# First block of a fused kernel: a longer distance from h to y, weights converted two chunks ahead, three passes from earlier chunks on

## The chip, the cores and the metric

The kernel runs on one core of a Trainium2 chip. Its metric is the device time of one execution in microseconds. TensorE multiplies matrices, VectorE, ScalarE and GpSimd do the elementwise work, and SyncE (SP) issues every DMA. Each engine works through its own instructions in order and waits on semaphores for the others.

## The reference

An attention with keys and values averaged over groups of 8 positions, and two feed-forward layers behind it, all float32 (2304 rows, 512 wide, 2048 hidden):

```python
k_p = k.reshape(B, H, Sp, 8, D).mean(axis=3)      # v_p likewise
attn = softmax(q @ k_p.T / sqrt(D))               # B 4, H 8, S 576, D 64
x = (attn @ v_p) as (2304, 512)
h = x @ w_in                                      # 512 -> 2048
g = where(h >= 1, h, where(h <= -1, 0, (h + 1)**2 / 4))
x = g @ w_out                                     # 2048 -> 512
h = x @ w_in2;  g = max(h, 0) + log1p(exp(-abs(h)));  out = g @ w_out2
```

## The kernel before

The 18 tiles of 128 rows are cut into blocks of 4, 4, 4, 3 and 3 tiles (`BLK`). Attention of a block's tiles runs one block ahead, among the matmuls of the block before; that of block 0 stands in a list, `START`. In each block the first feed-forward layer runs over 16 chunks of 128 hidden columns. The loop at L811 is this layer: turn n is chunk c of block j, here called step c. It emits h(c) = w_in(c) x on TensorE (`emit_g1`), then the elementwise g, and y += w_out(c) g (`emit_g2`) some steps later. `pend` holds the chunks whose y is still to come; before the change y runs two chunks behind h. The h banks in PSUM are two, so h(c) needs min/max(c-2), the last reader of its bank.

`act` makes g: Relu and Square on ScalarE, then min/max on VectorE (L538). A chunk that is multiplied in three passes has g split besides: a high half (ScalarE, L546) and a low half (VectorE, L548).

A product is made either in one fp32 pass, or in three passes of halves rounded to fp32r: high x high, high x low, low x high. For three passes w, x or g has to be split. `HSPLIT` says from which chunk of block 0 h takes three passes, `GSPLIT` the same for y. The later blocks take three throughout. `split_x0` splits the x of block 0 in two parts, `split1` a weight piece (ScalarE first, VectorE a step later), `SPLITS` says in which step.

The weights come as 64-bit words. `convert1` turns one piece of two chunks' weights into fp32 in two parts: two ScalarE passes (`words`), then two on VectorE (`exponents`: a shift, L125, and a merge, L126) and one on GpSimd (`last_bits`, L132). `USE` is the order of the 16 pieces: w_in of chunks 0 and 1, w_in of 2 and 3, w_out of 0 and 1, w_in of 4 and 5, w_out of 2 and 3, and so on. `w_load` brings a piece by DMA, four steps ahead.

`background` adds what `plan` has for each half step hs = 2n and 2n+1: the k and v sums of the next batch (L348), their transposes (L399) and scaled copies (L355, L359), and the stages of an attention tile (`tile_gen`): scores, row minimum, exponentials, normalisation, transposes, product with v, copy into x. A "wide" tile subtracts the minimum on VectorE and has one exponential of 576 columns, others eight of 72. From CONV2 on `tick` adds the conversion of the second layer's weights. The order on each engine is the order in which this code is run.

Of the kernel before, what the change touches and what calls it, by code (L numbers as in the profile page):

```python
# [25 lines left out]
NC = DFF // 128  # L26
# [4 lines left out]
def pooled_attention_ffn_ffn(ctx, tc, q, k, v, v0, w1, w2, out):  # L31
# [11 lines left out]

    START = (
        "z z z z z k0 k1 k2 k3 q0 q1 q2 q3 v w0 w1 K0 K1 K2 K3 L A0 A1 A2 B0 E0 B1 E1 A3 V C0 B2 D0 "
        "B3 E2 E3 T0 C1 U W0 C2 D1 P0 C3 T1 X0 D2 P1 S0 T2 X1 D3 P2 F0 T3 X2 P3 X3 w2 W1 b w3"
    )


# [6 lines left out]
    )  # L56


    HSPLIT, GSPLIT = 8, 12
    CONV2, PITCH = 44, 3.1  # L60

    BUDGET = ((0.0, 0.0), (1.0, 2.5), (1.2, 2.5), (0.9, 1.9), (0.9, 1.9))
    T0 = [sum(BLK[:j]) for j in range(NB)]
# [46 lines left out]
    def slot(shape, dtype, name):  # L110
        return wpool.tile(shape, dtype, tag="w", name=name)
# [5 lines left out]
    def words(src, a, r):  # L117
        x = src.rearrange("p (f w) -> p f w", w=2)
        nc.scalar.activation(
            out=a.bitcast(FP32), in_=x[:, :, 1].bitcast(FP32), func=ACTF.Copy, scale=2.0 ** -112  # L120
        )
        nc.scalar.activation(out=r, in_=x[:, :, 0], func=ACTF.Copy, scale=2.0 ** -29)

    def exponents(a, b):
        nc.vector.tensor_scalar(out=b, in0=a, scalar1=3, scalar2=None, op0=ALU.logical_shift_left)  # L125
        nc.vector.scalar_tensor_tensor(  # L126
            out=a, in0=a, scalar=0x80000000, in1=b, op0=ALU.bitwise_and, op1=ALU.bitwise_or
        )

    def last_bits(a, r):  # L130
        a = a.bitcast(I32)
        nc.gpsimd.tensor_tensor(out=a, in0=a, in1=r, op=ALU.add)  # L132
# [10 lines left out]
    def convert1(m):  # L143
        a = slot([128, 2 * DM], U32, "wf")
        r = es2.cv.tile([128, 2 * DM], I32, tag="r", name="r")
        words(raw.pop(m), a, r)
        yield
        b = es2.cv.tile([128, 2 * DM], U32, tag="b", bufs=1, name="b")
        exponents(a, b)
        last_bits(a, r)  # L150
        wt[USE[m]] = a.bitcast(FP32).rearrange("p (h f) -> p h f", h=2)
        yield
        yield

    def split1(m):

        hi, lo = (slot([128, 2, DM], FP32R, n) for n in ("whi", "wlo"))
        f = wt[USE[m]]
        nc.scalar.activation(out=hi, in_=f, func=ACTF.Copy)
        yield  # L160
        nc.vector.tensor_tensor(out=lo, in0=f, in1=hi.bitcast(FP32), op=ALU.subtract)
        wt[USE[m]] = (hi, lo)
        yield

    def st_load(n):
        if n < 2 * NC:
            (part, h), r = USE[n // 2], n % 2
            raw[n] = es2.cv.tile([128, 2 * DM], U32, tag="st", name="st")
            landing.append([3, n])
            src = w2[part, h].bitcast(U32)[:, r * 2 * DM:(r + 1) * 2 * DM]  # L170
            nc.sync.dma_start(out=raw[n], in_=src)
# [167 lines left out]
    def kv_load(b, nm, p, ring=True):  # L339
        shape = [128, T * POOL]  # L340
        t = es2.cv.tile(shape, FP32, tag="kv", name="kv") if ring else slot(shape, FP32, "kv")
        nc.sync.dma_start(out=t, in_=k[b, p] if nm == "k" else v[b - 1, p])
        kst[b, nm, p] = t
# [13 lines left out]
    def v_done(b, pa):  # L357
        vps[b] = att.tile([T, DM], FP32, tag="vp", bufs=2, name="vp")
        nc.scalar.activation(out=vps[b], in_=pa[0:T, 0:DM], func=ACTF.Copy, scale=1.0 / POOL)  # L359
# [211 lines left out]
    def emit_y(j):  # L571
        n = 128 * BLK[j]
        t = xpool.tile([128, KD, TB], FP32, tag="xh", name="y")
        for m, y in enumerate(yacc.pop(j)):
            if m % 2:
                nc.vector.tensor_copy(out=t[:, m, 0:n], in_=y[:, 0:n])
            else:
                nc.scalar.activation(out=t[:, m, 0:n], in_=y[:, 0:n], func=ACTF.Copy)  # L578
        later.append((j, t))
# [97 lines left out]
    c1 = [convert1(m) for m in range(NC)]  # L677
# [39 lines left out]
    for op in START.split():  # L717
        n = int(op[1:] or 0)
        if op == "z":
            for _ in range(4):  # L720
                nc.tensor.matmul(out=zp, lhsT=zeros[:, 0:128], rhs=zeros, start=True, stop=True)
        elif op == "b":
            for nm in "kv":
                for p in range(NP):
                    kv_load(1, nm, p, ring=False)
        elif op == "v":
            v0_load()
        elif op == "V":
            vpa = v0_pool(ps_z.tile([128, 512], FP32, tag="zp", name="vpa"))
        elif op == "U":  # L730
            v_done(0, vpa)
        elif op == "L":
            k_done(0)
        elif op[0] == "k":
            kv_load(0, "k", n, ring=False)
        elif op[0] == "K":
            kv_pool(0, "k", n)
        elif op[0] == "w":
            w_load(n)
        elif op[0] == "q":  # L740
            q_load(n)
        elif op[0] in "WSF":
            next(c1[n])
        else:
            if op[0] == "A":
                tg[n] = tile_gen(n, 0, wide=n != 1)
            next(tg[n])
# [5 lines left out]


    def wide(i):
        return i >= T0[2] and i % 2 == 0

    plan = {}
    for j, counts in enumerate(KV_PLAN):
# [15 lines left out]
    def background(hs):  # L775
        credit[0] = min(credit[0] + BUDGET[hs // 2 // NC][hs % 2], 3.0)
        for key in plan.get(hs, ()):
            if key not in gens:
                gens[key] = (
                    kv_gen(key[1]) if key[0] == "kv" else x_gen(key[1]) if key[0] == "x"  # L780
                    else tile_gen(*key, wide=wide(key[0]))
                )
            credit[0] -= cost.get(key, 0.0)
            cost[key] = next(gens[key])
        if hs >= CONV2:
            todo = len(units)
            tick(hs >= due[0])
            due[0] += (len(units) < todo) * PITCH

    pend = []  # L790
    acts = {}
    SPLITS = {
        (0, 13): (14,),
        (0, 14): (15, 0),
        (0, 15): (1, 2),
        (1, 1): (3,),
        (1, 2): (4,),
        (1, 3): (5,),
        (1, 4): (6,),
        (1, 5): (8,),  # L800
        (1, 6): (10,),
        (1, 7): (12,),
    }
    splits = []

    def step(key):

        if key in acts:
            next(acts[key], None)

    for n in range(NB * NC):  # L811
        j, c = s = divmod(n, NC)
        hs = 2 * n
        hot = j == 0
        if s == (1, 0):
            esc.close()
            es2.cv = esc.enter_context(tc.tile_pool(name="cv2", bufs=2))
        acts[n] = act(emit_g1(j, c), j, c)
        pend.append(s)

        if hot and c + 2 < NC:
            next(c1[c + 2])
        if n > NC + 2:
            step(n - 2)
        step(n - 1)
        if j and c == 2:
            emit_y(j - 1)
        for g in splits:
            next(g)
        splits = []  # L830
        if n <= NC + 2:
            step(n - 2)
        if hot and c + 1 < NC:
            next(c1[c + 1])
        if hot and c in (HSPLIT - 2, HSPLIT - 1):
            xg = split_x0(c - HSPLIT + 2)
            next(xg)

        if hot and HSPLIT - 1 <= c < NC - 2 and c % 2:
            w0 = split1(c)  # L840
            next(w0)
        if hs == CONV2 - 4:
            st_load(0)
            st_load(1)
        background(hs)

        while later:
            y1_store(*later.pop(0))
        while len(pend) > 2:
            emit_g2(*pend.pop(0))  # L850
        step(n - 1)
        next(acts[n])
        if hot and c + 1 < NC:
            next(c1[c + 1])
        if hot and c + 4 < NC:
            w_load(c + 4)
        if hot and c in (HSPLIT - 2, HSPLIT - 1):
            next(xg, None)
        if hot and HSPLIT - 1 <= c < NC - 2 and c % 2:
            next(w0)  # L860
        background(hs + 1)

        if (j, c) in SPLITS:
            splits = [split1(m) for m in SPLITS[j, c]]
            for g in splits:
                next(g)
            credit[0] -= 1.2
        if j == LAST and c in (11, 12, 13, 14):
            for i in range(2):
                wi_load((c - 11) // 2, (c - 11) % 2 * 2 + i)  # L870
# [13 lines left out]
    NQ = NS * NH  # L884
    xg = None

    FILL = {0: (2, 2, 1, 1, 1, 1, 0), 1: (0, 0, 0, 0, 0, 0, 6), NQ - 1: (0,) * 7}

    def filler(n):
        for _ in range(min(n, len(fill))):  # L890
# [3 lines left out]
    for q in range(NQ):  # L894
# [7 lines left out]
        if m == 2 and s + 1 < NS:  # L902
            xg = x_gen(s + 1)
        for p, o in enumerate(banks[b] for b in PRODUCTS):
# [11 lines left out]
            if p == 6:  # L916
                act2(q, 1, hb)
            filler(FILL[q][p] if q in FILL else 2 if p < 5 else 1)
            while later:
# [49 lines left out]
```

## Time and profile before

| | us |
|---|---|
| median of 3 runs | 874.84 (874.32 to 874.99) |
| the profiled execution | 875.78 |
| its span, first to last instruction | 874.0 |
| TensorE busy in the span | 860.2 (98%) |
| VectorE, ScalarE, GpSimd busy | 580.9, 517.8, 86.8 |
| first block, from its first h to its last | 28 to about 136 |

Rows of the profile begin with a start and a duration, or with a stretch. In the windows every engine has busy time and count; behind them stand TensorE's granted clock (1.00 is full), the share of the DMA engines and GB/s. The names before and behind `<-` are tiles written and read; brackets at a row's end give the idle time ahead of it and what ended it. In the chain a piece of fp32 matmuls counts two records each. L numbers are lines of the kernel before.

### The profile page before, as it was taken

To read this page: it belongs to the slowest core of one execution; us is meant where nothing else is said; L and a number is where in the kernel's file an instruction comes from. 1 tells how busy PE (TensorE), PEld (TensorE's weight loads), DVE (VectorE), ACT (ScalarE), POOL (GpSimd) and SP (SyncE) were. 2 spreads that over 40 slices of the span, in tenths; PEclk is the share of its full clock that TensorE was granted. 3 is DMA by queue.
4 is the path that set the end of the run, shared out by engine and by line. 5 is a ranking of instruction groups with operands and counts; after the bars stand their busy time and mean duration, and the time that the engine had idled before them with its cause. 6 is when DMAs were issued, how large, how long until landed. Compare 5 with 4: busy or idle time off the path is not lost.

```text
span 874.0 us, 12211 instructions
## 1 busy us (share of the span) xinstructions
PE 860.2 (98%) x4538; PEld 721.9 (83%) x4538; DVE 580.9 (66%) x845; ACT 517.8 (59%) x931; POOL 86.8 (10%) x57
## 2 busy tenths in 40 slices
PE   8999999999999999999999999999999999999997
PEld 4445668888887888899999988998898989989886
DVE  6577666755576475667675487767687675765754
ACT  4877765565656665777674457455475554644552
POOL 0442330011111112112110000000000000000000
PEclk9999999999999999999999999999999999999999
DMA  7853401512386353754867395556296455596302
GB/s 265 331 181 150 157 13 42 177 37 89 121 273 212 126 169 109 241 176 140 275 235 240 116 340 181 165 171 252 89 392 214 115 177 217 184 353 198 94 1 73
DMA packets 65643, 154.94 MB, mean 177 GB/s; under 512 B 6128, under 2 KB 26608, under 8 KB 63536
## 3 DMA queue, kind: packets, MB, share of 16 engines
q1 hardware_dynamic: 65584, 154.17, 52.2%
q8 instruction: 36, 0.59, 0.3%
q14 instruction: 23, 0.19, 0.1%
HBM read 121.63 MB, written 32.51 MB: 176 GB/s over the span
## 4 chain that ended last, share of the span: by engine, by line
PE 91%; ACT 3%; DMA 3%; DVE 2%; issue 1%; SPq 0%; ACTq 0%
PE h L523 22%; PE y L564 22%; PE y L640 22%; PE h L603 19%; PE a L412 2%; PE a L470 2%; PE a L456 2%; DMA x<-y1d 1%; DMA st<-in_w 1%; DMA kv<-in_k 1%; ACT e L445 1%; PE vpa L374 1%; ACT pT L462 0%; DVE e L452 0%; DVE mn L431 0%
## 5 line engine op out<-in xcount | busy, mean ns | idle before, releaser
L603 PE MATMUL h<-xfh,wi 128*128 128x384 f32 x544 | 160.3, 337 | 1.9 <-DVE h L911 1.2
L640 PE MATMUL y<-whi,gl 128*128 128x512 f32 x288 | 114.2, 397 | 0.4 <-DVE gl L624 0.4
L523 PE MATMUL h<-xl,whi 128*128 128x512 f32 (+1 forms) x320 | 114.3, 373 | 0.0
L640 PE MATMUL y<-wlo,gh 128*128 128x512 f32 x288 | 113.7, 395 | 0.0
L640 PE MATMUL y<-whi,gh 128*128 128x512 f32 x288 | 112.0, 389 | 0.0
L603 PEld LDWEIGHTS h<-xfh,wi 128*128 128x128 f32 x544 | 100.8, 188 | 9.4 <-DVE h L911 2.6
L564 PE MATMUL y<-gh,whi 128*128 128x512 f32 (+1 forms) x272 | 100.9, 371 | 1.1 <-ACT y L578 1.1
L564 PE MATMUL y<-gl,whi 128*128 128x512 f32 (+1 forms) x272 | 99.0, 364 | 0.0
L564 PE MATMUL y<-gh,wlo 128*128 128x512 f32 (+1 forms) x272 | 98.9, 364 | 0.0
L523 PE MATMUL h<-xh,whi 128*128 128x512 f32 (+1 forms) x256 | 94.1, 368 | 0.0
L523 PE MATMUL h<-xh,wlo 128*128 128x512 f32 (+1 forms) x256 | 92.8, 362 | 0.0
L603 PE MATMUL h<-xfl,wi 128*128 128x384 f32 x272 | 91.8, 338 | 0.0
L614 ACT ACTIVATE e<-h 128x768 f32<-128x768 f32 x48 | 40.1, 840 | 84.9 <-DVE h L911 84.9
L532 ACT ACTIVATE t<-h 128x512 f32<-128x512 f32 (+1 forms) x80 | 44.3, 554 | 74.7 <-PE h L523 74.6
L911 DVE TENSOR_TENSOR h<-h,s 128x384 f32<-128x384 f32 x72 | 40.0, 555 | 65.5 <-PE h L603 65.1
L132 POOL TENSOR_TENSOR a<-a,st 128x512 int32<-128x512 int32 x32 | 47.4, 1483 | 275.5 <-DVE a L126 194.2
L538 DVE SCALAR_TENSOR_TENSOR t<-t,h 128x512 f32<-128x512 f32 (+1 forms) x68 | 42.2, 620 | 41.9 <-ACT t L533 41.8
L523 PEld LDWEIGHTS h<-xl,whi 128*128 128x128 f32 x320 | 59.8, 188 | 8.4 <-issue 1.4
L640 PEld LDWEIGHTS y<-whi,gl 128*128 128x128 f32 x288 | 54.0, 187 | 12.3 <-DVE gl L624 0.8
L640 PEld LDWEIGHTS y<-whi,gh 128*128 128x128 f32 x288 | 54.1, 188 | 6.3
L640 PEld LDWEIGHTS y<-wlo,gh 128*128 128x128 f32 x288 | 54.0, 187 | 6.3
L564 PEld LDWEIGHTS y<-gh,whi 128*128 128x128 f32 x272 | 51.0, 188 | 8.5 <-ACT y L578 1.4
(96 smaller groups left out, 1630.9 us busy)
## 6 DMA issues: line engine op xcount, KB each, us to landing
wi<-wid SPq DMA_DIRECT2D x72, 512.0 KB, 5.8
raw<-in_w SPq DMA_DIRECT2D x16, 1024.0 KB, 4.9
st<-in_w SPq DMA_DIRECT2D x32, 512.0 KB, 4.1
whi<-wod SPq DMA_DIRECT2D x24, 512.0 KB, 4.0
wlo<-wod SPq DMA_DIRECT2D x24, 512.0 KB, 5.0
wid<-b SPq DMA_DIRECT2D x24, 256.0 KB, 4.0
wi<-wid SPq DMA_DIRECT2D x24, 256.0 KB, 5.4
kv<-in_k SPq DMA_DIRECT2D x16, 288.0 KB, 3.7
```

Of the source, the lines that this page charges most:

```text
L132: nc.gpsimd.tensor_tensor(out=a, in0=a, in1=r, op=ALU.add)
L412: nc.tensor.matmul(out=pa[off:off + n, r * 512 + p * T:r * 512 + (p + 1) * T], lhsT=qt[rows, p, off:off + n], rhs=kps[b][rows, p, :], star ...
L456: nc.tensor.transpose(pa[0:T, h * 128:(h + 1) * 128], e3[:, h, :], ident)
L470: nc.tensor.matmul(out=pa[r * D:(r + 1) * D, p * 128 + off:p * 128 + off + n], lhsT=vps[b][:, h * D:(h + 1) * D], rhs=pT[:, c0:c0 + n], st ...
L523: nc.tensor.matmul(out=h, lhsT=a, rhs=b, start=(done == 0), stop=(done == len(ops) * KD - 1),)
L532: nc.scalar.activation(out=g, in_=h, func=ACTF.Relu, bias=1.0)
L538: nc.vector.scalar_tensor_tensor(out=g, in0=t, scalar=1.0, in1=h, op0=ALU.min, op1=ALU.max)
L564: nc.tensor.matmul(out=y[:, 0:128 * BLK[j]], lhsT=a, rhs=b, start=(c == 0 and n == 0), stop=(c == NC - 1 and n == len(ops) - 1),)
L603: nc.tensor.matmul(out=o, lhsT=a[:, cols], rhs=b[:, kk, :], start=(p in FRESH and done == 0), stop=(done == 5), skip_group_check=True,)
L614: nc.scalar.activation(out=e, in_=h, func=ACTF.Abs)
L640: nc.tensor.matmul(out=y, lhsT=a, rhs=b, start=(m == w == n == 0), stop=(last and n == 2))
L911: nc.vector.tensor_tensor(out=h, in0=o, in1=keep[x], op=ALU.add)
```

## The change

The diff, whole but for the plain context:

```diff
-        "B3 E2 E3 T0 C1 U W0 C2 D1 P0 C3 T1 X0 D2 P1 S0 T2 X1 D3 P2 F0 T3 X2 P3 X3 w2 W1 b w3"
+        "B3 E2 E3 T0 C1 U W0 C2 D1 P0 C3 T1 X0 D2 P1 S0 T2 X1 D3 P2 T3 X2 P3 X3 w2 W1 b S1 w3"
...
-    HSPLIT, GSPLIT = 8, 12
+    HSPLIT, GSPLIT = 4, 8
...
         wt[USE[m]] = a.bitcast(FP32).rearrange("p (h f) -> p h f", h=2)
         yield
-        yield
...
     def wide(i):
-        return i >= T0[2] and i % 2 == 0
+        return i in (5, 7) or i >= T0[2] and i % 2 == 0
...
+    LAG = 3
...
     SPLITS = {
-        (0, 13): (14,),
-        (0, 14): (15, 0),
...
+        (0, 2): (3,),
+        (0, 4): (5,),
...
-        if hot and c + 2 < NC:
-            next(c1[c + 2])
-        if n > NC + 2:
-            step(n - 2)
+        step(n - 2)
         step(n - 1)
-        if j and c == 2:
+        if j and c == LAG:
             emit_y(j - 1)
-        for g in splits:
-            next(g)
-        splits = []
-        if n <= NC + 2:
-            step(n - 2)
-        if hot and c + 1 < NC:
-            next(c1[c + 1])
-        if hot and c in (HSPLIT - 2, HSPLIT - 1):
-            xg = split_x0(c - HSPLIT + 2)
-            next(xg)
-
-        if hot and HSPLIT - 1 <= c < NC - 2 and c % 2:
-            w0 = split1(c)
-            next(w0)
         if hs == CONV2 - 4:
             st_load(0)
             st_load(1)
         background(hs)
+        if hot and c + 2 < NC:
+            next(c1[c + 2])
+        for g in splits:
+            next(g)
+        step(n - 2)
+        if hot and c in (HSPLIT - 2, HSPLIT - 1):
+            xg = split_x0(c - HSPLIT + 2)
+            next(xg)
 
         while later:
             y1_store(*later.pop(0))
-        while len(pend) > 2:
+        while len(pend) > LAG:
             emit_g2(*pend.pop(0))
-        step(n - 1)
         next(acts[n])
-        if hot and c + 1 < NC:
-            next(c1[c + 1])
+        if hot and c in (HSPLIT - 2, HSPLIT - 1):
+            next(xg, None)
+        if hot and c + 2 < NC:
+            next(c1[c + 2])
         if hot and c + 4 < NC:
             w_load(c + 4)
-        if hot and c in (HSPLIT - 2, HSPLIT - 1):
-            next(xg, None)
-        if hot and HSPLIT - 1 <= c < NC - 2 and c % 2:
-            next(w0)
         background(hs + 1)
 
+        splits = []
         if (j, c) in SPLITS:
...
-    FILL = {0: (2, 2, 1, 1, 1, 1, 0), 1: (0, 0, 0, 0, 0, 0, 6), NQ - 1: (0,) * 7}
+    FILL = {0: (3, 3, 2, 2, 1, 1, 0), 1: (0, 0, 0, 0, 0, 0, 6), NQ - 1: (0,) * 7}
```

In words: y runs three chunks behind h. Both parts of converting piece c+2 stand in step c, the first behind `background(2n)` and the second ahead of `background(2n+1)`; before, the first part of piece c+2 stood at the head of step c and the second in step c+1. Pieces 3, 5, 7, 9, 10 to 15 and 0 are split in steps 2 to 15 of block 0, one at a time, and 1, 2, 4, 6, 8 in block 1. x is split in steps 2 and 3 (before: 6 and 7). h takes three passes from chunk 4, y from chunk 8. Tiles 5 and 7 are wide. The high half of g is made at the head of step c+2 and the low half in its middle; before, at the end of step c+1 and the head of step c+2.

On TensorE, at the start of block 0, the rows before are these (h(0) to h(2), then y(0), then h(3)):

```order
L523 MATMUL h<-xh,wf 128x512 x12
L564 MATMUL y_436<-g,wf 128x512
L564 MATMUL y_437<-g,wf 128x512
L564 MATMUL y_438<-g,wf 128x512
L564 MATMUL y_439<-g,wf 128x512
L523 MATMUL h<-xh,wf 128x512 x4
```

With the change, at the same place (the scores of tile 4 are `a<-kp,q`, and h(4) follows them):

```order
L522 MATMUL h<-xh,wf 128x512 x16
L563 MATMUL y_469<-g,wf 128x512
L563 MATMUL y_470<-g,wf 128x512
L563 MATMUL y_471<-g,wf 128x512
L563 MATMUL y_472<-g,wf 128x512
L411 MATMUL a<-kp,q 64x72 x16
L522 MATMUL h<-xl,whi 128x512 x2
L522 MATMUL h<-xl,wlo 128x512
```

h(3) has moved ahead of y(0), and h(4) is in three passes.

On VectorE around the last v sums (`ks<-kv`) and the row minimum of tile 4 (`mn`), before:

```order
L126 SCALAR_TENSOR_TENSOR wf_455<-wf_455,b_507 128x1024
L348 TENSOR_REDUCE ks_467<-kv_362 128x72
L431 TENSOR_REDUCE mn_514<-a_479 128x8
L348 TENSOR_REDUCE ks_467<-kv_364 128x72
L538 SCALAR_TENSOR_TENSOR g_545<-t_530,h_496 128x512
```

And with the change:

```order
L537 SCALAR_TENSOR_TENSOR g_519<-t_477,h_452 128x512
L347 TENSOR_REDUCE ks_461<-kv_362 128x72
L430 TENSOR_REDUCE mn_524<-a_489 128x8
L125 TENSOR_SCALAR b_547<-wf_536 128x1024
L126 SCALAR_TENSOR_TENSOR wf_536<-wf_536,b_547 128x1024
L347 TENSOR_REDUCE ks_461<-kv_364 128x72
```

The shift and merge of a weight piece (`b_547`, `wf_536`) now stand between the row minimum and the last v sum.

On ScalarE at the eight exponentials of tile 4 (`e,sm<-a,mn`), before:

```order
L119 ACTIVATE wf_501<-raw_447 128x1024
L122 ACTIVATE r_502<-raw_447 128x1024
L445 ACTIVATE e_516,sm_515<-a_479,mn_514 128x72 x8
L532 ACTIVATE t_530<-h_496 128x512
L533 ACTIVATE t_530<-t_530 128x512
```

And with the change:

```order
L531 ACTIVATE t_477<-h_452 128x512
L532 ACTIVATE t_477<-t_477 128x512
L444 ACTIVATE e_526,sm_525<-a_489,mn_524 128x72 x8
L119 ACTIVATE wf_536<-raw_446 128x1024
L122 ACTIVATE r_537<-raw_446 128x1024
```

The conversion passes (`wf<-raw`, `r<-raw`) of this step have moved from ahead of the exponentials to behind them.

## Rows read from the trace of the kernel before

**Rows 1.** Busy time of each engine from 28 to 136 us, clock, DMA.

```profile
28.00:136.00 108.00, 106.93 (x465) 60.29 (x464) 77.74 (x83) 76.80 (x147) 35.60 (x15) 1.00 0.43 156
```

**Rows 2.** TensorE's waits, 28 to 136 us, then 260 to 380: total, times, longest.

```profile
PE a L456 <- DVE e L452: 1.1, 1, 1.1
...
PE y L564 <- ACT y L578: 1.1, 1, 1.1
PE a L470 <- ACT pT L462: 0.3, 1, 0.3
```

**Rows 3.** Chain that ended last, in order of time: start, us, what.

```profile
27.74 10.54 PE h L523 x24
...
41.73 3.43 PE h L523 x8
...
102.70 2.73 PE h L523 x12
...
138.92 2.72 PE h L523 x12
```

**Rows 4.** TensorE's timeline, the transposes of v: start, us, instruction, idle before.

```profile
59.60 0.60 PE L399 MATMUL a<-ident,ks 128*72 128x128 f32 x4
```

**Rows 5.** ScalarE's timeline: start, us, instruction, idle before.

```profile
35.08 1.15 ACT L119 ACTIVATE wf<-raw 128x1024 f32<-128x1024 f32 x1 [2.20 <-DMA raw<-in_w]
...
37.17 0.59 ACT L532 ACTIVATE t<-h 128x512 f32<-128x512 f32 x1
...
38.33 1.14 ACT L119 ACTIVATE wf<-raw 128x1024 f32<-128x1024 f32 x1
...
44.62 0.43 ACT L355 ACTIVATE kp<-ks 128x288 f32<-128x288 f32 x1
...
51.02 0.32 ACT L445 ACTIVATE e<-a,mn 128x72 f32<-128x72 f32 x1 [1.95 <-DVE mn L431]
...
53.40 0.63 ACT L532 ACTIVATE t<-h 128x512 f32<-128x512 f32 x1
...
60.96 0.57 ACT L359 ACTIVATE vp<-a 72x512 f32<-72x512 f32 x1
...
63.54 1.04 ACT L504 ACTIVATE xl<-xh 128x1024 fp32r<-128x1024 f32 x1
64.54 1.02 ACT L462 ACTIVATE pT<-a 72x1024 f32<-72x1024 f32 x1
```

**Rows 6.** VectorE's timeline.

```profile
38.45 0.69 DVE L538 SCALAR_TENSOR_TENSOR g<-t,h 128x512 f32<-128x512 f32 x1 [1.67 <-ACT t L533]
39.06 0.69 DVE L125 TENSOR_SCALAR b<-wf 128x1024 uint32<-128x1024 uint32 x1
39.78 1.22 DVE L126 SCALAR_TENSOR_TENSOR wf<-wf,b 128x1024 uint32<-128x1024 uint32 x1
40.92 1.41 DVE L348 TENSOR_REDUCE ks<-kv 128x72 f32<-128x576 f32 x2
...
47.16 1.23 DVE L125 TENSOR_SCALAR b<-wf 128x1024 uint32<-128x1024 uint32 x1
...
50.23 0.75 DVE L431 TENSOR_REDUCE mn<-a 128x8 f32<-128x576 f32 x1
...
87.98 3.13 DVE L161 TENSOR_TENSOR wlo<-wf,whi 128x1024 fp32r<-128x1024 f32 x1 [0.57 <-ACT whi L159]
```

**Rows 7.** GpSimd's timeline.

```profile
45.47 2.37 POOL L132 TENSOR_TENSOR wf<-wf,r 128x1024 int32<-128x1024 int32 x1 [1.96 <-DVE wf L126]
...
87.63 2.40 POOL L132 TENSOR_TENSOR wf<-wf,r 128x1024 int32<-128x1024 int32 x1 [3.79 <-DVE wf L126]
```

**Rows 8.** Windows after the last matmul: busy times, granted clock, DMA.

```profile
872.00:873.00 1.00, 0.00 (x0) 0.00 (x0) 0.00 (x0) 0.00 (x0) 0.00 (x0) 1.00 0.60 227
873.00:874.00 1.00, 0.00 (x0) 0.00 (x0) 0.00 (x0) 0.00 (x0) 0.00 (x0) 0.58 0.00 0
```

**Rows 9.** TensorE's timeline, the first matmuls.

```profile
1.25 6.91 PE L721 MATMUL zp<-zeros 128*128 128x512 bf16 x20 [1.25 <-DVE zeros L663]
```

More of the change, by code (lines that the diff above doesn't have):

```diff
@@ L741, in pooled_attention_ffn_ffn @@
             q_load(n)
-        elif op[0] in "WSF":
+        elif op[0] in "WS":
             next(c1[n])
@@ L792, in pooled_attention_ffn_ffn @@
     SPLITS = {
+        (0, 2): (3,),
+        (0, 4): (5,),
+        (0, 6): (7,),
+        (0, 8): (9,),
+        (0, 9): (10,),
+        (0, 10): (11,),
+        (0, 11): (12,),
+        (0, 12): (13,),
         (0, 13): (14,),
-        (0, 14): (15, 0),
-        (0, 15): (1, 2),
-        (1, 1): (3,),
+        (0, 14): (0,),
+        (0, 15): (15,),
+        (1, 0): (1,),
+        (1, 1): (2,),
         (1, 2): (4,),
[L798 to L802, printed above, removed]
+        (1, 3): (6,),
+        (1, 4): (8,),
     }
```

## The prediction, made before the changed kernel was run

> **What bounds the kernel now.** I read the busy times by stretch, then TensorE's waits, then the chain, then the timelines of the four engines over the first block. In the first block TensorE is busy 106.93 of 108 us, VectorE 77.74 and ScalarE 76.80 [rows 1]: matmuls set the pace, and what a matmul saves is kept only if no other engine then makes TensorE wait. It waits little: 1.1 us for a normalisation in this block, and 1.1 and 0.3 us at two places of the later ones [rows 2]. One chunk's h or y as a single fp32 pass stands for 3.43 us in the chain, one in three passes for 2.72 to 2.73 [rows 3]: 0.70 us a chunk. Block 1 begins at 138.92 [rows 3]; then h(0) to h(15) and y(0) to y(13) are done. I count chunks and steps from 0.
>
> **What the change removes.** h(4) to h(7) and y(8) to y(11) go from one pass to three: 8 x 0.70 = 5.6 us less on TensorE. If the normalisation is no longer late, 1.1 us more goes. So 6.7 us is to be had in the first block.
>
> **What it adds and moves there.** The number of weight halves split stays 16; four more of them fall into the first block and two leave it. Four chunks more have g split (a ScalarE copy and a VectorE subtraction of 128x512 each). Two tiles trade eight short exponentials on ScalarE (51.02 to 53.40, 2.38 us [rows 5]) for VectorE work and one long one. In the totals there is room for that. The order is what matters: VectorE and ScalarE run their queues in order, and the conversions are now placed behind the attention work of their step. I followed these queues by hand from 35.08, where ScalarE has waited for the DMA of the fourth weight piece [rows 5]; the change does not touch what is ahead of that piece, so this time stays. Costs are start to start: conversion on ScalarE 2.09 (35.08 to 37.17), Relu and Square 1.16 (37.17 to 38.33), x split 1.00 (63.54 to 64.54) [rows 5]; on VectorE min/max 0.61, exponent shift 0.72, exponent merge 1.14, a k or v sum 0.67 (half of two, less the overlap), row minimum 0.75 [rows 6]; GpSimd's last bits 2.37, and a shift or subtraction that meets it waits for its end: the shift at 47.16 took 1.23 against 0.69 and ended 0.55 after GpSimd, the subtraction at 87.98 took 3.13 and ended 1.08 after it [rows 6, 7].
>
> Step 1. Relu and Square of chunk 1 end at 38.4, and min/max(1) at 39.5 (VectorE first finishes the exponents and a k sum that begins about 38.1). Its h bank is the one that h(3) needs. Before, y(0) stood between h(2) and h(3) and hid this; now h(3) comes right behind h(2), which ends at 38.28 (27.74 + 10.54 [rows 3]): wait 1.2. It can't be below 0; the upper end is 2.2, if an exponent shift falls behind GpSimd one piece earlier.
>
> Steps 2 and 3. TensorE would reach h(4) at 39.5 + 3.43 + 3.43 + 0.7 (scores) = 47.1. ScalarE: conversion 4 to 40.4, x split to 41.5, Relu, Square, and a weight split to 43.6. VectorE: low half of x 41.5 to 42.6, exponents(4) to 44.5, k sum to 45.2; then ScalarE's k copy (0.43 [rows 5]) to 45.7 and conversion 5 to 47.8, second x split to 48.8. GpSimd works 44.7 to 47.1, so the low half of weight 3 ends at 48.2, and the second low half of x at 50.05. h(4) wants the one at its third matmul and the other at its eighth: two waits, 0.6 and 0.9, and h(4) ends at 51.2 in place of 49.85. Together 1.4.
>
> Steps 4 and 5. y(1) and h(5) run to 57.4. VectorE from 50.05: exponents(5) to 51.9, v sum, min/max(3), v sum, row minimum to 54.55. Then eight exponentials to 57.0 on ScalarE, and only then conversion 6, whose first half ends at 58.1. VectorE has nothing to do from 54.55 to 58.15, since exponents(6) stand at the head of its queue and the last v sum behind them: exponents to 60.0, v sum to 60.75. For that sum wait TensorE's transposes of v, and behind them y(2) and all else. Before, that sum was done at 51.6 (right behind the row minimum at 50.23 [rows 6]) and the transposes ran at 59.60 without waiting [rows 4]. Now they can start at 60.8: wait 3.4. This is the largest term and the least safe. From below it is 0, if the queues run 3.4 us ahead of my times; from above I take 4.5, one more collision of a shift with GpSimd (2.37 less what overlaps). Waits in steps 1 to 3 do not add to it: TensorE's later arrival only moves part of it.
>
> Steps 5 to 7. The transposes of e need the bank that the v copy (0.57, the 60.96 row [rows 5]) empties at 65.05, against 64.7: 0.4. The next tile's scores wait for its low half of x, queued behind GpSimd until 73.65, against 73.35: 0.3. Another 0.15 of that kind in step 12. For the two copies of x the Trainium skill, page "SBUF — State Buffer", section "Who interferes with whom", says that an operation of VectorE with at most one operand in SBUF, outside its two-port modes, does not contend with GpSimd; x's low half reads one operand from PSUM. No run here shows such a pair; by that rule the 0.3 goes and the sum is 0.3 us lower.
>
> From step 8 the two engines have caught up: their results are there two to three us before TensorE asks, e.g. the low half of weight 11 at 107.3 for h(12) at 109.5, the last norm at 126.0 for its transposes at 128.7. So a term taken out of the early steps is won only up to about 2 us before the later ones bind. Adding the matmul durations from 61.25 on gives h(15) at 132.3, y(12) at 136.35 and y(13) at 139.1, the point that stands at 138.92 before: **0.2 us later**. As a sum: -6.7 + 1.2 + 1.4 + 3.4 + 0.4 + 0.3 + 0.15 = +0.15.
>
> **The other blocks.** y now lags by three, so the high half of g is taken a whole step after min/max and TensorE asks for the low half one step later: both looser. ScalarE's high half, first in its step, waits for the y that frees its buffer, but that y ends before the transposes, which anything behind it needs. The wait for y's copy at the block's change (1.1 [rows 2]) came of eight exponentials and a conversion ahead of the copy; with the change of blocks one step later, the exponentials stand a step earlier and it should go. The 0.3 behind a conversion that waits for its DMA I leave, and I add 0.3 for one new wait of that size: -0.8, from -1.4 to +1.5. The twelve leftover pieces of y instead of eight are the same matmuls in another place: 0, with TensorE busy on both sides as cover. SP's loads and stores are the same ones, some a step later.
>
> **Sum.** The profiled execution took 875.78 us, 1.78 around a span of 874.0. The span becomes 874.0 + 0.2 - 0.8 = 873.4, the execution 875.2; the median of the runs is 0.94 lower, so **874.2**.
>
> **Rivals.** *The full saving.* The early queues hold TensorE up by little, as rows 1 suggest (30 us free on either engine), and only h(3) and one to two us besides remain: 874.8 - 6.7 + 1.2 + 1.5 - 0.8 = 870.0; half-way cases lie about 872. For it: one early operation that I put behind GpSimd and isn't frees up to 2 us. Against it: the idle stretch of VectorE at 54.55 comes of the order alone. *The clock falls.* If the wait for the transposes of v grows past 4 us, TensorE's clock may drop. After the last matmul the granted clock is still 1.00 in the window to 873, four us of idleness, and 0.58 (between full and half) in the next [rows 8]; the longest wait inside the kernel now is 1.1 to 1.3. What it costs is seen at the start: 20 warm-up matmuls took 6.91 us [rows 9], at 2.72 / 12 = 0.227 each [rows 3] they would take 4.5: 2.4 us. With one us more of waiting, 874.2 + 1.1 + 2.4 = 877.7, slower. Against it: 3.4 is short of that. The Trainium skill, page "TensorE: Matmul & The Clock Gate", section "HAM oscillation — how this bites in real kernels", has idle gaps throw a kernel back to the slow clock; by it this stall might cost the 2.4 without growing, 876.6. *ScalarE behind a DMA.* A conversion of the second weights that waits for its load in another step would hold the high half and Relu behind it; the before shows 0.3 of it; at one us in each of three blocks 877.
>
> **Chances.** Runs differ by 0.7 us, and about 0.2% (1.75 us) is what a measurement here can tell from nothing: faster is under 873.1, slower over 876.6. My forecast, with its own range 872.7 to 875.9, 0.48; full or half saving 0.34; clock 0.08; DMA 0.10. Faster 0.35, same 0.46, slower 0.19. The range takes in the better part of the saving and the smaller losses: 870.7 to 877.0.
>
> **What would show it.** In the after: h(3) waiting about 1 us for VectorE's min/max, two short waits inside h(4), and the transposes of v waiting about 3 us for the v sum, with VectorE idle ahead of an exponent shift and ScalarE in its eight exponentials just before. Each chunk named above at 2.72; no wait for y's copy at 350; granted clock 1.00 near 61. I am wrong if the transposes of v start below 59, if TensorE's waits in the first block sum to less than 4 us, or if new waits of over 2 us stand in blocks 1 to 4.

## The result and the profile after

The changed kernel took 879.87 us (median of 4 runs, 878.97 to 882.66), the kernel before 874.91 beside it: ratio 1.0061, 95% interval 1.0049 to 1.0073. It is slower by about 5 us and lies outside the range that was given. The profiled execution took 879.55 us with a span of 877.8, against 874.0.

Three marks with equal work done show where the 3.8 us of span arose. h(0) begins at 27.42 after and 27.74 before (-0.32). The product that follows on h(0) to h(15) and y(0) to y(13), or as many products, begins at 140.23 after and 138.92 before, so the first block lost 1.63. The first product of the second layer begins at 485.44 after and 484.06 before; allowing for the one y of 2.08 us that is left over in addition, it comes another 2.15 later, and the second layer adds 0.34. The rows of these marks, the chain and TensorE's timeline after, then the timeline before:

```profile
140.23 2.72 PE y L563 x12
```

```profile
485.44 0.33 PE L602 MATMUL h<-xfh,wi 128*128 128x384 f32 x1
```

```profile
484.06 0.33 PE L603 MATMUL h<-xfh,wi 128*128 128x384 f32 x1
```

The whole first block in one window after (stretch, length, busy PE, PEld, DVE, ACT, POOL, granted clock, DMA share, GB/s):

```profile
28.00:136.00 108.00, 102.33 (x491) 65.42 (x490) 84.69 (x97) 77.09 (x125) 36.28 (x15) 0.98 0.43 155
```

TensorE is idle for 5.7 us where it was idle for 1.1, and its mean clock is 0.98 [rows 1]; VectorE has 7 us more to do. TensorE's timeline there (start, us, instruction, idle before and what ended it):

```profile
27.42 7.11 PE L522 MATMUL h<-xh,wf 128*128 128x512 f32 x16 [0.79 <-ACT xh L482]
35.17 3.67 PE L522 MATMUL h<-xh,wf 128*128 128x512 f32 x8 [0.64 <-DVE g L537]
40.07 3.70 PE L522 MATMUL h<-xh,wf 128*128 128x512 f32 x8 [1.23 <-DVE g L537]
...
49.84 0.50 PE L522 MATMUL h<-xl,whi 128*128 128x512 f32 x1 [0.17 <-DVE xl L506]
...
57.33 0.49 PE L398 MATMUL a<-ident,ks 128*72 128x128 f32 x3
60.52 0.30 PE L398 MATMUL a<-ident,ks 128*72 128x128 f32 x1 [2.71 <-DVE ks L347]
```

These answer to [rows 3, 4]. The first bracket, 0.79, stands before too; the others are new waits: h(2) and h(3) for min/max, h(4) for x's low half, and the last transpose of v for the last v sum, where before all four ran at 59.60 without a wait. Three of the four ran at 57.33; only the last was late.

VectorE and ScalarE ahead of that sum, after:

```profile
53.49 0.75 DVE L430 TENSOR_REDUCE mn<-a 128x8 f32<-128x576 f32 x1
57.85 0.69 DVE L125 TENSOR_SCALAR b<-wf 128x1024 uint32<-128x1024 uint32 x1 [3.62 <-ACT wf L119]
58.58 1.23 DVE L126 SCALAR_TENSOR_TENSOR wf<-wf,b 128x1024 uint32<-128x1024 uint32 x1
59.72 0.75 DVE L347 TENSOR_REDUCE ks<-kv 128x72 f32<-128x576 f32 x1
```

```profile
54.27 0.32 ACT L444 ACTIVATE e<-a,mn 128x72 f32<-128x72 f32 x1 [4.59 <-DVE mn L430]
...
56.66 1.16 ACT L119 ACTIVATE wf<-raw 128x1024 f32<-128x1024 f32 x1
```

VectorE sits idle for 3.62 us with the sum in its queue, because the shift ahead of it waits for ScalarE's conversion, which stands behind the eight exponentials [rows 5, 6].

Windows around it, and the chain (start, us, what):

```profile
61.00:62.00 1.00, 1.00 (x2) 0.34 (x1) 1.00 (x2) 1.00 (x2) 1.00 (x1) 0.50 1.05 442
...
64.00:65.00 1.00, 1.00 (x4) 0.51 (x3) 1.00 (x2) 0.61 (x2) 0.00 (x0) 0.88 0.76 147
```

```profile
60.52 0.30 PE a L398
60.83 5.13 PE y L563 x8
```

Behind the wait the granted clock is 0.50, which is 1.2 GHz, for some three us. y(2) takes 5.13 us where the same product took 3.43 [rows 3]: 1.7 us that no wait shows.

Waits by the later blocks, 140 to 440 us (us in total, times, longest), TensorE's after and then ScalarE's over the whole span:

```profile
PE a L469 <- ACT pT L461: 2.4, 3, 1.3
PE a L455 <- DVE e L451: 1.0, 1, 1.0
```

```profile
ACT t L531 <- DVE gl L547: 43.4, 26, 4.5
ACT gh L545 <- PE y L563: 40.3, 38, 2.7
```

Before, TensorE waited 1.1 for y's copy and 0.3 for pT there [rows 2]; these are gone, and 3.4 us of others stand in their place: 0.83 at 170.44, 1.32 at 381.57, 1.02 at 399.73 and 0.27 at 403.18. ScalarE before waited 10.5 us for y (15 times) and never for the low half `gl`. The chain of the first of the new waits, after:

```profile
161.36 0.52 ACT gh L545
...
164.89 1.14 DVE wlo L160
166.03 0.61 DVE gl L547
...
166.75 0.61 ACT t L531
...
167.38 0.63 ACT t L532
168.01 0.95 ACT whi L158
168.96 0.52 ACT gh L545
169.48 0.92 ACT pT L461
...
170.44 1.09 PE a L469 x16
```

Relu (L531) may write its buffer only when the low half that reads it is made. That low half comes four us behind its high half, since a normalisation and a weight split stand ahead of it in VectorE's queue. Relu waits, and behind it in ScalarE's queue wait Square, a weight split, the high half and at last pT, for which TensorE has been idle 0.83 us at 170.44.

### The profile page after: what moved, and what is told of

It is laid out like the page before. It is cut to its first block, busy times and chain, and to the rows that moved or that the text cites. A ratio compares the mean times of both kernels' runs of the same rounds, so it can differ in the third digit from the quotient of the medians.

```text
span 877.8 us, 12295 instructions
## 1 busy us (share of the span) xinstructions
PE 857.4 (98%) x4570; PEld 728.2 (83%) x4570; DVE 591.5 (67%) x855; ACT 515.5 (59%) x905; POOL 84.3 (10%) x57
## 4 chain that ended last, share of the span: by engine, by line
PE 86%; ACT 6%; DVE 5%; DMA 1%; issue 1%; SPq 0%; ACTq 0%
PE y L639 23%; PE y L563 20%; PE h L602 19%; PE h L522 18%; PE a L411 2%; PE a L469 2%; PE a L455 1%; ACT e L444 1%; ACT wf L119 1%; DMA wid<-b 1%; PE zp L720 1%; ACT r L122 1%; ACT pT L461 1%; DMA raw<-in_w 1%; DVE wf L126 1%
## 5 line engine op out<-in xcount | busy, mean ns | idle before, releaser
L522 PE MATMUL h<-xl,whi 128*128 128x512 f32 (+1 forms) x352 | 124.8, 376 | 0.2 <-DVE xl L506 0.2
L602 PEld LDWEIGHTS h<-xfh,wi 128*128 128x128 f32 x544 | 100.7, 188 | 10.6 <-DVE h L906 2.6
L563 PE MATMUL y<-gh,whi 128*128 128x512 f32 (+1 forms) x288 | 107.2, 372 | 0.0
L563 PE MATMUL y<-gl,whi 128*128 128x512 f32 (+1 forms) x288 | 105.2, 365 | 0.0
L563 PE MATMUL y<-gh,wlo 128*128 128x512 f32 (+1 forms) x288 | 105.2, 365 | 0.0
L531 ACT ACTIVATE t<-h 128x512 f32<-128x512 f32 (+1 forms) x80 | 44.3, 554 | 95.8 <-PE h L522 49.1
L537 DVE SCALAR_TENSOR_TENSOR t<-t,h 128x512 f32<-128x512 f32 (+1 forms) x72 | 45.0, 624 | 49.3 <-ACT t L532 49.0
L522 PEld LDWEIGHTS h<-xl,whi 128*128 128x128 f32 x352 | 65.5, 188 | 10.2 <-issue 1.4
L132 POOL TENSOR_TENSOR a<-a,st 128x512 int32<-128x512 int32 x32 | 44.2, 1382 | 301.4 <-DVE a L126 227.4
L545 ACT ACTIVATE gh<-t 128x512 fp32r<-128x512 f32 (+1 forms) x72 | 41.7, 579 | 40.9 <-PE y L563 40.3
L563 PEld LDWEIGHTS y<-gh,whi 128*128 128x128 f32 x288 | 54.0, 188 | 7.9 <-issue 1.5
L547 DVE TENSOR_TENSOR gl<-t,gh 128x512 fp32r<-128x512 f32 (+1 forms) x72 | 47.6, 662 | 19.0 <-ACT gh L545 19.0
```

Of the source, the lines that this page charges most:

```text
L522: nc.tensor.matmul(out=h, lhsT=a, rhs=b, start=(done == 0), stop=(done == len(ops) * KD - 1),)
L531: nc.scalar.activation(out=g, in_=h, func=ACTF.Relu, bias=1.0)
L537: nc.vector.scalar_tensor_tensor(out=g, in0=t, scalar=1.0, in1=h, op0=ALU.min, op1=ALU.max)
L545: nc.scalar.activation(out=gh, in_=g, func=ACTF.Copy)
L547: nc.vector.tensor_tensor(out=gl, in0=g, in1=gh.bitcast(FP32), op=ALU.subtract)
L563: nc.tensor.matmul(out=y[:, 0:128 * BLK[j]], lhsT=a, rhs=b, start=(c == 0 and n == 0), stop=(c == NC - 1 and n == len(ops) - 1),)
```

## The experiments

Ratios are to the kernel before, run beside each; its medians were 875.54, 875.92 and 875.21 us in the three groups of runs. Theory: the first block's 2.7 us wait and the clock behind it come of the words standing behind the attention work, and the later blocks' loss of the halves of g coming late.

**Words ahead of the attention work (e1).**

```diff
-        background(hs)
         if hot and c + 2 < NC:
             next(c1[c + 2])
+        background(hs)
```

> The changed kernel, with the first half of each conversion of block 0 (two ScalarE passes) ahead of the attention work of its step again, and nothing else. Theory (order of the queues): conversion 6 no longer stands behind the eight exponentials, so VectorE's exponent merge and the last v sum behind it end near 56.8 instead of 60.4; TensorE's wait for the v sum goes from 2.7 us to under 0.5, the granted clock stays at 1.00 around 61 and y(2) takes 3.43 instead of 5.13 us. About 3 us less than the changed kernel: 876.5 to 877.5. Rival (the engines have too much work in the first steps, whatever the order): another wait of 2 to 3 us takes its place within the next steps and the time stays within 1 us of 879.9.

875.82 us, ratio 1.0003 (0.9994 to 1.0012). The wait for the v sum is gone. TensorE's waits, 28 to 140, and one window:

```profile
PE h L522 <- DVE g L537: 2.5, 2, 1.9
PE a L455 <- ACT vp L358: 1.3, 1, 1.3
```

```profile
62.00:63.00 1.00, 0.30 (x1) 0.00 (x0) 0.97 (x2) 0.97 (x2) 0.00 (x0) 1.00 0.26 41
```

One pair of lines exchanged gives back nearly the whole loss, one us or more above what was expected. There is now a wait of 1.3 us for the v copy, and the clock stays at 1.00 through it and through one of 1.9 for min/max.

**Matmuls in the wait (e4).** 14 products of zeros stand ahead of the transposes of v; nothing else is changed.

```diff
+        for _ in range(14 if b == 1 else 0):
+            nc.tensor.matmul(out=pa[:, 0:512], lhsT=zeros[:, 0:128], rhs=zeros, start=True, stop=True)
```

> The changed kernel, with 14 matmuls on zeros added ahead of the transposes of v in block 0; they write a part of the bank that the transposes and what follows overwrite or don't read. Theory (the idle time let the clock fall): TensorE is busy in the wait, the granted clock stays at 1.00 and y(2) takes 3.43 instead of 5.13; the v sum comes at the same 60.4, and since the next wait (v copy, near 65.1) takes back a part, about 1 us less than the changed kernel: 878.5 to 879.3. Rival (the clock fell for another reason, such as the denser work before): it falls again, y(2) takes about 5 us, time 879.5 to 880.5.

878.11 us, ratio 1.0034 (1.0022 to 1.0046). TensorE's timeline and one window:

```profile
58.34 3.20 PE L398 MATMUL a<-zeros 128*128 128x512 bf16 x13
61.38 0.60 PE L400 MATMUL a<-ident,ks 128*72 128x128 f32 x4
61.81 3.60 PE L565 MATMUL y<-g,wf 128*128 128x512 f32 x8
```

```profile
61.00:62.00 1.00, 1.00 (x8) 0.78 (x7) 1.00 (x3) 1.00 (x3) 0.95 (x1) 1.00 0.31 115
```

The transposes come no sooner, yet the clock stays at 1.00 and y(2) lasts 3.60 in TensorE's timeline, where it lasted 5.30 in the changed kernel. The kernel is 1.8 us faster by the medians, 2.4 by the ratios. The trace does not put this down to the clock. The transposes of e behind y(2) wait 0.31 for the v copy and begin at 65.73, in the changed kernel at 65.80, and the product that begins at 140.23 there begins at 140.22 here. In this execution h(0) itself ran in part at 0.50 (29:31) and the fourth weight piece came 1.0 us later, which hides up to that much. The second layer begins 1.42 earlier, because the wait of 1.32 at 381.57 is missing, far from the edit.

**Low half made early (e3), and with e1 (e5).** The low half stands right behind min/max at the head of step c+2.

```diff
         step(n - 1)
+        step(n - 2)
         if j and c == LAG:
...
-        step(n - 2)
```

> The changed kernel, with the low half of g (VectorE) made right behind min/max, ahead of the step's attention work, conversions and weight splits, and nothing else. Theory (buffer of t): Relu of chunk n waits for the low half of chunk n-2, since t has two buffers; with the low half early, ScalarE's wait of Relu for it (43.4 us in total in the changed kernel, none before) shrinks below 15, and TensorE's waits for pT and for the normalised e in blocks 1 to 4 (3.4 us) go below 1: 877.0 to 878.0. Rival (the high half first in the step, waiting for y, delays pT): the waits for pT stay at 2 us or more and the time stays at 879 to 880.

883.45 us, ratio 1.0095 (1.0082 to 1.0108): slower still. In 140 to 440 the waits for pT fall to 0.2 us, but 4.8 us for the norm come up. VectorE's timeline:

```profile
397.51 0.56 DVE L547 TENSOR_TENSOR gl<-t,gh 128x384 fp32r<-128x384 f32 x1 [3.05 <-ACT gh L545]
```

Now VectorE is held by the high half, 56.2 us in 140 to 440 against 12.0 in the changed kernel: moving the low half moves the wait to the other engine. The longer of the two waits for the norm, 2.92, has a DMA in its chain: a conversion starts when its load lands, at 375.13, and the high half follows at 377.10.

> The changed kernel with both edits: conversions first in the step, low half of g right behind min/max. If the two causes are separate, the gains add: 5 to 6 us less than the changed kernel, 873.5 to 875.5, about the time of the kernel before. If they are one (ScalarE late in either place because of Relu's wait), the two together bring no more than the better one alone, 876 to 877.5.

881.19 us, ratio 1.0061 (1.0038 to 1.0084). The two edits don't add up. In the trace the waits for the norm (3.9 us) stay; but the profiled execution, 876.75, is the fastest of six that reach to 885.41, so what the slower ones waited for isn't shown.

**Old order and distance from block 1 on (e7), and with e1 (e6).**

```diff
+        if n == NC:
+            step(n - 2)
         step(n - 2)
         step(n - 1)
-        if j and c == LAG:
+        if j and c == 2:
             emit_y(j - 1)
+        if n >= NC:
+            for g in splits:
+                next(g)
+            splits = []
...
-        step(n - 2)
+        if n < NC:
+            step(n - 2)
...
-        while len(pend) > LAG:
+        while len(pend) > (LAG if n < NC else 2):
             emit_g2(*pend.pop(0))
+        if n >= NC:
+            step(n - 1)
...
-    FILL = {0: (3, 3, 2, 2, 1, 1, 0), ...
+    FILL = {0: (2, 2, 1, 1, 1, 1, 0), ...
```

> The changed kernel, only with the order of the kernel before from block 1 on (y two chunks behind h there); block 0 as changed. Theory: 2.5 us less than the changed kernel, 877.0 to 878.0, with the 2.7 us wait for the v sum and the clock at 0.5 behind it still there. Rival: no gain, 879 to 880.5.

877.63 us, ratio 1.0016 (1.0006 to 1.0025), with the v sum's wait of 2.8 us in place. The clock that was expected at 0.5 behind it stayed at 1.00 (55:75), y(2) lasted 3.60, and the v copy was waited for, 0.41. TensorE's timeline:

```profile
62.54 0.31 PE L398 MATMUL a<-ident,ks 128*72 128x128 f32 x1 [2.77 <-DVE ks L347]
```

> The changed kernel with conversions first in the step (as in e1_conv_first), and from block 1 on the order of the kernel before: y two chunks behind h, high half of g at the end of the step behind min/max, low half at the head of the next. Theory (in the later blocks the high half, first in its step, waits for the y that frees its buffer, one step later than before, and holds up ScalarE and, through the low half and t, VectorE): the later blocks go back to the 1 to 2 us of waits they had before, and the start of the second layer too; about 2.5 us less than e1_conv_first: 872.5 to 874.0. Rival (the waits of blocks 1 to 4 come from the changed places of the weight splits and second-layer conversions): no gain over e1, 875 to 876.5.

873.30 us, ratio 0.9974 (0.9963 to 0.9985): faster than both kernels. By the ratios the later blocks' order is worth 3.9 us on the changed kernel (1.0061 to 1.0016) and 2.5 on e1 (1.0003 to 0.9974); the traces of the changed kernel and the one before had put 2.15 to 2.5 on it, the second layer included.

**Distance alone (e12) and order alone (e13), from block 1 on.** e12 takes only the lines with LAG and FILL of the diff above, e13 only those that move the two halves.

> The changed kernel with y two chunks behind h from block 1 on, the places of the halves of g as changed. If the late high half comes of the lag (with y three chunks behind, the buffer of the high half comes free a step later and ScalarE waits for that y): the waits of Relu for the low half and of the high half for y shrink to those of the kernel before (4.5 and 40 us in all in the changed kernel, none and 10.5 before), the waits of TensorE for pT and the norm in blocks 1 to 4 go, 877 to 878. If it comes of the place of the halves in the step alone: they stay, 879.5 to 881, more if TensorE now waits for low halves.

894.44 us, ratio 1.0213 (1.0189 to 1.0237).

> The changed kernel with the two halves of g back at their old places from block 1 on (high at the end of the next step, low at the head of the one behind it), y still three chunks behind h. If the lag is the cause: the high half still waits for y, now right behind the product that frees its buffer, Relu for the low half likewise: as slow as the changed kernel or slower, 879.5 to 883. If the place of the halves is the cause: 877 to 878.

920.35 us, ratio 1.0508 (1.0484 to 1.0532). Neither of the two answers that I had set against each other came out. e12's waits of TensorE, then e13's of ScalarE, 140 to 440:

```profile
PE y L563 <- DVE gl L547: 7.0, 10, 2.4
PE y L563 <- ACT gh L545: 2.5, 2, 1.7
```

```profile
ACT gh L545 <- PE y L563: 126.1, 39, 9.2
```

In e12 the halves, in the middle of the step, are late for a y that is now asked for in the same step; ScalarE's wait for y, 34.6 us there in the changed kernel, is no longer among its largest there (down to 1.5). TensorE's waits there, 10.6 us in all, are a part of the 15.8 that e12 loses on the changed kernel up to the second layer; the rest wasn't followed. In e13 the high half, at the end of the step, stands right behind the y that frees its buffer, and ScalarE is held 126 us. So distance and place hold each other: with two buffers for the high half and y three behind, the old place costs 126 us of ScalarE's time, and the later place with its small waits is the price. A third buffer, which would test it in one edit, wasn't tried.

e13's first block has the changed kernel's code and the same wait, and its clock stayed at 1.00 (55:75). TensorE's timeline and the chain:

```profile
61.49 0.30 PE L398 MATMUL a<-ident,ks 128*72 128x128 f32 x1 [2.74 <-DVE ks L347]
61.63 3.60 PE L563 MATMUL y<-g,wf 128*128 128x512 f32 x8
```

```profile
140.16 2.72 PE y L563 x12
```

From h(0), at 27.55, to this mark it took 112.61 us, the changed kernel 112.81. So the fallen clock lengthened y(2) by 1.7 us but the block by only 0.2: with the clock up, TensorE waits where it otherwise comes late: 0.43 for the v copy, and later for x's low half as before.

**Three passes earlier in the old order: y from 8 (e8), h from 6 too (e9), wide tiles too (e10).**

```diff
-    HSPLIT, GSPLIT = 8, 12
+    HSPLIT, GSPLIT = 8, 8
...
+        (0, 9): (10,),
+        (0, 11): (12,),
...
-        (1, 6): (10,),
-        (1, 7): (12,),
```

e9 has `HSPLIT` 6 and drops `(1, 3): (5,)`; e10 also has `i in (5, 7)` in `wide`.

> The kernel before with one part of the change alone: y in three passes from chunk 8 instead of 12, with the two weight pieces for it split in steps 9 and 11; order, lag and all else as before. Theory (the saving is real and the new order lost it): 4 x 0.70 = 2.8 us less on TensorE and under 1 us of new waits: 872.0 to 873.5. Rival (ScalarE and VectorE have no room in the first block, so that every split put there becomes a wait): 874.5 or more.

877.26 us, ratio 1.0021 (1.0005 to 1.0037): slower, the rival's answer. TensorE waits 1.2 and 2.2 us for the norm of two tiles, and the clock is 0.83 in 130:140.

> As e8_old_y8, and h in three passes from chunk 6 instead of 8 (x split in steps 4 and 5, one more weight piece in step 5). Theory: 6 x 0.70 = 4.2 us less on TensorE and 1 to 2 us of new waits: 871.5 to 873.0. Rival (no room): worse than e8_old_y8, 874.5 or more.

875.44 us, ratio 0.9999 (0.9987 to 1.0010). Both waits remain. e9's chain around the second (this execution took 878.78 and began h(0) at 30.98, some 3.3 us later than the others):

```profile
121.46 2.53 ACT e L445 x16
...
129.11 1.23 DVE wf L126
...
130.69 2.76 DVE e L452
...
133.50 1.54 PE a L456 x8
135.04 3.88 PE h L523 x12
```

Eight exponentials, then a conversion's merge, then a norm that meets GpSimd (2.76 in place of 0.77 without), then eight transposes and h at a fallen clock (0.50 in 134:136).

> The old order with three passes from h chunk 6 and y chunk 8, as in the run before it, and tiles 5 and 7 wide as well. That run kept two waits of TensorE for a normalisation, 1.20 at 110 and 2.18 at 133, and a clock of 0.83 in 130:140. Theory: both come of the eight short exponentials of tiles 5 and 7, 2.4 us on ScalarE; with the wide form they go, the clock stays at 1.00, and the time is 871.5 to 873. Rival: they come of the added splits of weights, and ScalarE and VectorE have no room whichever form the tiles take: waits of 2 us or more remain in 100:140 and the time is 874.5 to 876.

872.17 us, ratio 0.9964 (0.9950 to 0.9979). The time is the one expected of the theory, but not by its way: two waits of 1.2 and 2.1 us remain, and the clock still falls behind the longer, ahead of which the scaling of 128x8 (`sm`) now meets GpSimd (1.85, where it takes 0.17 without):

```profile
125.92 1.85 DVE sm L450
...
128.94 1.89 PE a L456 x8
130.83 3.50 PE h L523 x12
```

Wide tiles help here, but which of the instructions they move gives the 3 us stays open.

**Narrow tiles in the fastest so far (e11).** e6 with `wide` as before.

> The fastest version so far (words ahead of the attention work in the first block, the old order from block 1 on), with tiles 5 and 7 in the narrow form again. Theory that the wide form carries the gain of the early passes at the end of the block: waits for a normalisation of 1 to 2 us each come back near 110 and 133, and the time rises by 2 to 4 us to 875.5 to 877. Rival, that the new order has room for the eight exponentials: no such wait over 0.5, 873 to 874.

871.83 us, ratio 0.9962 (0.9943 to 0.9981), no wait for a norm in the first block. The rise that the theory wanted didn't come; the interval overlaps that of e6, so that narrow tiles are better isn't shown, only that wide ones aren't needed with the words in front. e11 has the lowest time, 3.3 us under before by its ratio; e10 can't be told from it.

## Why the prediction was wrong

The span was forecast at 873.4 and came at 877.8. Of these 4.4 us, 1.4 arose in the first block, 2.95 in the other blocks and 0.34 in the second layer; the start gave 0.32 back. The rest of the miss in the median is its place: I put it 0.94 under the profiled execution, and it lay 0.32 above.

**What is removed: right in kind, its size a failed step.** Products in three passes mostly take 2.72 to 2.77 in the chain (2.94 behind scores or a product with v, as before), and the first block has no wait for the norm left. e6 and e11, which keep these passes and lose the new waits, are below the kernel before. But "8 x 0.70 = 5.6 us less on TensorE" came out as 4.7, the fallen clock set aside, and as 4.2 in e13 (below).

**Steps 1 to 3: right in sum, not in their terms.** h(3) waited 1.23 for min/max (1.2 forecast), h(2) 0.64 (none forecast), h(4) 0.17 (1.4). Not all of the rest was saved: in the timeline h(0) and h(1) took 7.11 in place of 6.86, h(2) 3.67 in place of 3.43, and h(4) 3.34 from its first matmul to y(1). From h(0) to y(2) the changed kernel took 33.41 us, and my working had 33.5. The point I began from, ScalarE at the fourth weight piece, does not stay: with the same code ahead of it, it lay at 34.86 after and at 36.87 in e7, where h(3) waited 2.61.

**Steps 4 and 5: right.** VectorE idle from 54.55 to 58.15 was forecast, 54.23 to 57.85 came; the v sum ready at 60.75, it was 60.48; a wait of 3.4, it was 2.71. Following the three queues by hand gave these times good to 0.4 us.

**The clock: a condition that failed, a cost that hardly counted.** The rival put it that the clock may drop "if the wait for the transposes of v grows past 4 us", and against it "3.4 is short of that". In the changed kernel it fell in 2.71, against my sign "granted clock 1.00 near 61". My bound came from the end of the trace [rows 8], an idle stretch with the DMA at work and nothing behind it, which isn't a wait between matmuls. The Trainium skill, page "TensorE: Matmul & The Clock Gate", section "HAM oscillation — how this bites in real kernels", says that idle gaps throw a kernel back to the slow clock; the trace agrees, with 0.50 after 2.71 us, shorter than the waits of the section's example. Such a wait doesn't always do it: behind 2.77 in e7 and 2.74 in e13 the clock was 1.00, so its length alone doesn't decide. The price, 2.4 from the warm-up [rows 9], was 1.7 in y(2), of which e13 leaves 0.2 at the block's end. I had given this rival 0.08; its fall came, but it isn't what made the kernel slower.

**Steps 5 to 7: small terms, wrong.** The wait of 0.4 for the v copy did not come, since TensorE was later by the clock's 1.7; where the clock held it came, 0.41 in e7 and 0.43 in e13. One of 0.86 that I had not came at 117.70, scores of a tile for x's low half. The wait of 0.3 did not come either: the low half that I put behind GpSimd ran beside it:

```profile
71.62 0.69 DVE L485 TENSOR_TENSOR xl<-a,xh 128x512 fp32r<-128x512 f32 x1 [0.70 <-ACT xh L484]
```

```profile
71.14 2.37 POOL L132 TENSOR_TENSOR wf<-wf,r 128x1024 int32<-128x1024 int32 x1 [2.03 <-ACT t L532]
```

For operands of this kind the Trainium skill's page "SBUF — State Buffer", section "Who interferes with whom", had no contention, and the trace agrees: 0.69 with GpSimd busy throughout.

**The first block's sum.** The mark was due at 139.1 and came at 140.23. With the start 0.32 earlier, 1.63 us were lost from h(0) on where my working has 0.2. In the changed kernel TensorE's waits came to 5.7 us, 1.2 less than the 6.85 of my working, the saving to 0.9 less, and the clock took 1.7. In e13, with the clock up, the loss is 1.43 and the waits 6.7, near the forecast; what is missing is the saving, 4.2 in place of 5.6. A product with another right behind it lasts 3.60 in the timeline, whose ends are modelled, and is followed after 3.43; ahead of a wait that overlap of 0.17 is lost. For the seven waits that e13 has more, this makes 1.2 of the missing 1.4, an estimate from these rows. My working charged each wait its idle time alone.

**The other blocks: the larger failed step.** Forecast -0.8, measured +2.15. The wait for y's copy went as foreseen. But "both looser" was read off the distance between an operation and its user and left out the buffers. I wrote that the high half "waits for the y that frees its buffer, but that y ends before the transposes, which anything behind it needs", and had no word for Relu, whose buffer the later low half now holds: 43.4 us of ScalarE's waits, none before.

In the chain at 170.44 it is this that makes pT late, and at 403.18 again (Relu idle 2.79 before it), 1.1 us together; in e3, with the low half early, the waits for pT are down to 0.2, and others come. The high half's own wait for y grew too, but does not show in the chains of the four waits; e13 shows what it costs at the old place. Of the 1.02 at 399.73, 0.9 is the scaling of 128x8 on VectorE, which met GpSimd (1.07 in place of 0.17 at 397.57).

e7 and e6 undo the order and win 3.9 and 2.5 us; how that divides among the low half, the high half and the second layer is open.

The third rival, ScalarE behind a DMA, came true in one block: ScalarE's timeline and the chain, after,

```profile
374.81 0.63 ACT L239 ACTIVATE b<-a 128x512 fp32r<-128x512 f32 x1 [2.69 <-DMA wid<-b]
```

```profile
381.57 1.09 PE a L469 x16
```

In e4, with the same code in these blocks, that conversion waits 0.30 and begins at 372.40, and the product with v waits for nothing: the 1.32 us is the DMA's, in this execution. Without it the other blocks would stand at +0.8, still 1.6 above the forecast.

**The leftover y pieces, costed at nothing:** a wait of 0.78 for ScalarE's copy at 493.67 shows in the second layer, whose sum is 0.34. The traces with eight pieces again put more on it: less the y of 2.08, that layer took 390.3 in the changed kernel and 390.9 in e1, but 389.4 in e7 and e6, so 1.0 and 1.5 us of what those two win may lie there (one execution each). My own condition, "new waits of over 2 us stand in blocks 1 to 4", was met by their sum, 3.4; no single one was above 1.32.

## What to carry to other kernels

A longer distance between a product and its user buys slack only if the buffers between them grow with it; else the producer waits for the user's release, in order, with all that stands behind it. Follow the queues by hand for the first waits, and charge each wait also with the overlap that the product ahead of it loses. A wait of TensorE of the size seen here (2.1 to 2.8 us) may bring the slow clock, 1.6 to 1.7 us in the products behind it; what of that stays depends on whether they would have waited next anyway. Within a step, the conversion's words that other engines wait for go ahead of exponentials that nobody waits for yet.

## What the runs showed of the hardware

The clock fell to 0.50 behind waits of 2.71 us (after), 2.70 (e3), 2.73 (e12), 2.2 (e8, e9) and 2.1 (e10), each with TensorE nearly always busy ahead of it, and stayed at 1.00 through waits of 2.77 and 2.61 in e7, 2.74 in e13, and 1.9 and 1.3 in e1. In e4 it fell behind one of 0.79 ahead of h(0), with waits of 0.95 and less in the ten us before. That it stayed at 1.00 near 61 in e4, with products of zeros in place of the wait, therefore doesn't show that they held it. The loss was 1.7 us on y(2) and, in e9, 0.47 on eight transposes (1.54 in place of 1.07) and 1.13 on h (3.88 in place of 2.75).

Operations of VectorE that met GpSimd took longer: a normalisation 2.76 in place of 0.77 (e9), a scaling of 128x8 1.07 (after) and 1.85 (e10) in place of 0.17. The subtraction with one operand in PSUM was not held, 0.69.
